# Block 0's logits in a four-layer transformer kernel: half of the shifts on TensorE, half on VectorE

## The chip, the cores and the metric

The kernel runs on one core of a Trainium2 chip. The metric is the device time of one execution in microseconds, the median of the runs. The result is a bfloat16 tensor of 2048 rows by 1024 columns.

## The reference

Four layers work on x (2048 x 1024): attention, gated MLP, attention, gated MLP, each on a layernorm of x and added back to x. Both attention layers use the same weights, and so do both MLP layers.

```python
qkv = layernorm(x) @ wqkv            # 32 heads of 32
idx = pos[:, None] - 2 * arange(8)   # each row sees 8 rows: itself, 2, 4 .. 14 back
logits = einsum("bhsd,bhswd->bhsw", q, k[idx]) * scale   # -1e9 where idx < 0
x = x + einsum("bhsw,bhswd->bhsd", softmax(logits), v[idx]) @ wo
x = x + ((gate * (gate > 0)) * up) @ W_down   # gate, up = layernorm(x) @ W_gate, W_up
```

## The kernel before

The rows are cut into four blocks of 512 (four tiles of 128 rows each). Per layer and block there is a list of stages: layernorm; projections q, k, v; the attention proper; the output projection (wo) with its add to x; for the MLP the gate and up projections and the down projection. Layer indices in the code are 0 to 3, so `proj(0, b)` is the first attention.

**Who does what.** TensorE does all projections, as groups of eight matmuls of 128x512 into one PSUM bank (the pool has eight). ScalarE evicts the projections, takes the sums for the layernorm and normalises. VectorE does the attention, the adds to x and the product of the gated MLP. SP issues nearly all loads. ScalarE issues the writes of q, k and v to DRAM, and GpSimd those of the attention's output and of the 14 halo rows that the next block needs.

**Two layouts.** Projections come out feature-major: partitions are features, columns are rows of x. Attention on VectorE is head-major: partition 32*tq + h holds head h of row tile tq, the free dimension holds 32 features by 128 rows. The change of layout goes through DRAM (`q_d`, `k_d`, `v_d`, written by `evict`, read back in four pieces each as `qhm`, `khm`, `vhm` by `load`). Then `plan_attn` takes, for each of the eight shifts w, one product over 32 features (`mul`, L512) and its sum (`add3`, L522, and `fold`, L529 and L530); then softmax (`soft_a`, `expo`, `soft_b`); then eight steps over features with v (`pv_mul` L563, `pv_add` L571 to L574, which writes `o_d`); then `load_o` (L582) reads the result back, feature-major, as `oT` for the output projection (`plan_wo`, L642, adds at L649).

**Block 0 of layer 0 is special.** Its logits don't go through DRAM. `first_logits` keeps q and k feature-major in SBUF (`q_fm`, `k_fm`); VectorE multiplies each of the eight 128-feature chunks with all eight shifts of k in one instruction (`mul` in `first_logits`, L451), and TensorE sums the 32 features of each head by a matmul with a matrix of ones (`red`, L464; `wide` puts the sums in the right partitions). That is 32 matmuls for chunks 0 to 3 (placed after the first group of q1 by `step(0, 4)`) and 32 for chunks 4 to 7 (placed in block 1's projections by `step(4, 4)`). For this, block 0's projections run in the order q0 v0 k0 v1 q1 k1 (0 and 1 are the halves of 512 features); all others run q0 k0 q1 k1 v0 v1.

**What sets the order.** Instructions of each engine run in the order in which the program emits them. A planner (`Plan`) makes that order: every step gets a due time in us from fixed costs per kind, and steps are emitted by due time. TensorE's steps follow one another (`on_pe`, 0.216 us a matmul). VectorE's attention is one serial list over all blocks (`plan.chain`, each with a time from which it is ready and a cost), and adds and layernorm smalls are put between its entries (`on_dve`). Weight slabs of 512 columns go through a ring of five buffers on SP (`slab`). The due times only set the order; the waits are by semaphores. The six weight slabs of layer 0's projections are held through all four blocks.

In layer 0 the stages on TensorE are: projections of blocks 0, 1 and 2, wo of block 0, projections of block 3, then gate and up of block 0, wo of block 1, and so on.

Of the kernel before, what the change touches and what calls it, by code (L numbers as in the profile page):

```python
# [9 lines left out]
BF16 = mybir.dt.bfloat16  # L10
# [4 lines left out]
P = 128  # L15
# [3 lines left out]
W = 8  # L19
# [6 lines left out]
NEG = -1.0e9  # L26
SLAB = 512
ROW = HALO + BLK
DG = 4
RING = 5  # L30
NG = DH // DG


MM = 0.216
# [85 lines left out]
def kernel(  # L120
# [233 lines left out]
    def plan_proj(L, b, hooks={}):  # L354
# [33 lines left out]
        if L == 0 and b == 0:  # L388
# [4 lines left out]
            for t in range(TPB - 1):  # L393
                for h, (nm, g, j) in ((h, x) for h in range(2) for x in tiles):
                    plan.on_pe(1, mms(nm, g, j, w0[(nm, g)], t, t + 1, KC // 2 * h, KC // 2 * (h + 1)), [w0[(nm, g)]])
                    if h == 1 and j == 2:
                        e = plan.on_pe(2, lambda t=t: first.turn(t + 1))
                        plan.at(e, lambda t=t: first.copies(t + 1))
        order = "q0 k0 q1 k1 v0 v1" if "evict" not in hooks else "q0 v0 k0 v1 q1 k1"
        for nm, g in ((o[0], int(o[1])) for o in order.split()):  # L400
# [20 lines left out]
    def first_logits(st, tm):  # L421
        hold = {}
        Ls = []

        def begin():
            hold["q"] = hm_pool.tile([P, KC, BLK], BF16, tag="q", name="q_fm")
            hold["k"] = hm_pool.tile([P, KC, HALO + BLK], BF16, tag="k", name="k_fm")
            nc.gpsimd.memset(hold["k"][:, :, 0:HALO], 0.0)

        def evict(nm, c, acc, t):  # L430
            def f():
                if nm == "q":
                    nc.scalar.copy(hold["q"][:, c, :], acc()[:])
                    return
                kt = hold["k"]
                nc.scalar.copy(kt[:, c, HALO:HALO + BLK], acc()[:])
                nc.gpsimd.dma_start(_dram(k_d[1], c * P * ROW, [[ROW, P], [1, HALO]]), kt[:, c, BLK:BLK + HALO])
            if nm == "q" and c == 0:
                plan.at(t - 1.0, begin)
            plan.at(t, f)  # L440
            if nm == "k":
                plan.chain.append((lambda: max(t + 0.7, reds.get(c - 4, 0.0) + 0.1), 2.25, mul(c),
                                   (lambda n: tm.__setitem__("logits", n)) if c == KC - 1 else None))

        def mul(c):
            def f():
                if c % 4 < 2:
                    pr = at_pool.tile([P, W, BLK], BF16, tag="pr", name=f"prod_{c}", bufs=2)
                else:
                    pr = tpose.tile([P, W, BLK], BF16, tag="T", name=f"prod_{c}")  # L450
                nc.vector.tensor_tensor(pr[:], _ap(hold["q"], c * BLK, [[0, W], [1, BLK]]),  # L451
                                        _ap(hold["k"], c * ROW + HALO, [[-DIL, W], [1, BLK]]), op=ALU.mult)
                hold[("pr", c)] = pr
            return f

        def red(c0, n):
            def f():
                if c0 == 0:
                    Ls.extend(psum.tile([P, 4, P], F32, tag="acc", name=f"L{wh}") for wh in range(2))
                for c in range(c0, c0 + n):  # L460
                    pr = hold.pop(("pr", c))
                    for wh in range(2):
                        for tq in range(TPB):
                            nc.tensor.matmul(Ls[wh][32 * tq:32 * tq + 32, :, :], lhsT=wide[:, 28 - 4 * c:60 - 4 * c],  # L464
                                             rhs=pr[:, 4 * wh:4 * wh + 4, tq * P:(tq + 1) * P],
                                             start=(c == 0), stop=(c == KC - 1),
                                             skip_group_check=True, tile_position=(0, 32 * tq))
            return f

        def out():  # L470
            st["L"] = at_pool.tile([P, W, P], F32, tag="L", name="L_0_0")
            for wh in range(2):
                nc.scalar.copy(st["L"][:, 4 * wh:4 * wh + 4, :], Ls[wh][:])

        reds = {}

        def step(c0, n):
            def f():
                e = plan.on_pe(1.0 + 2.25 * n, red(c0, n))
                for c in range(c0, c0 + n):  # L480
                    reds[c] = e
                if c0 + n == KC:
                    plan.at(e + T_EV, out)
                    tm["logits_in"] = e + T_EV + 1.5
            return f

        return {"evict": evict, ("q", 1, 0): step(0, 4)}, {("q", 0, 2): step(4, 4)}


    def plan_attn(L, b, ends, st, tm):  # L490

        def load(t, parts):

            def piece(nm, src, row, n, tq):
                def f():
                    if tq == 0:
                        st[nm] = hm_pool.tile([P, DH, n], BF16, tag=nm, name=f"{nm}hm_{L}_{b}")
                    nc.sync.dma_start(st[nm][32 * tq:32 * tq + 32, :, :],
                                      _dram(src[b], tq * P, [[DH * row, H], [row, DH], [1, n]]))
                return f  # L500
            for p in parts:
                for tq in range(TPB):
                    plan.at(t, piece(*p, tq))
                    t += PIECE
            return t - PIECE + T_LAND

        def mul(w):
            def f():
# [79 lines left out]
        chain_tm.append(tm)  # L588

        def qk_ready():  # L590
            t = ends["k"] + 6.0
            if prev:
                t = max(t, prev[-1]["logits"] + 0.5)
            tm["qk_in"] = load(t, (("q", q_d, BLK, P), ("k", k_d, ROW, HALO + P)))
            return tm["qk_in"]

        def v_ready():
            t = ends["v"] + 6.0
            if prev:
                t = max(t, prev[-1]["pv"] + 0.5, tm["qk_in"] + 10.0)  # L600
            return load(t, (("v", v_d, ROW, HALO + P),))

        now = lambda: 0.0
        first = L == 0 and b == 0
        for w in range(0, 0 if first else W):
            plan.chain.append((qk_ready if w == 0 else now, 2.25, mul(w), None))
# [5 lines left out]
            plan.at(t + 0.2, expo)  # L612
            tm["exp"] = t + 2.2

        plan.chain.append(((lambda: tm["logits_in"]) if first else now, 3.0, soft_a, after_a))
# [85 lines left out]
    def plan_down(L, b, st, last):  # L701
# [21 lines left out]
        def add(half, t, c0, n):  # L723
            def f():
                xt = x_tiles[b * TPB + t]
                nc.vector.tensor_tensor(xt[:, c0:c0 + n], accs.pop((t, c0))[:], xt[:, c0:c0 + n], op=ALU.add)  # L726
                r0 = (b * TPB + t) * P
                if end:
                    eng = nc.scalar if t == 1 or (t == TPB - 1 and c0 == SLAB) else nc.sync
                    eng.dma_start(out_dram[r0:r0 + P, c0:c0 + n], xt[:, c0:c0 + n])  # L730
                elif last and half == 1:
                    nc.sync.dma_start(out_dram[r0:r0 + P, :], xt[:])
            return f

        for half in range(2):
# [13 lines left out]
    wo_start = []  # L749
    attn = {}  # L750
    glu = {}
    later_hooks = []

    def proj(L, b):
        st, tm = {}, {}
        if L == 0 and b == 0:
            hooks, later_hooks[:] = (lambda h: (h[0], [h[1]]))(first_logits(st, tm))
# [20 lines left out]
    for i, (nm, g) in enumerate((("q", 0), ("v", 0), ("k", 0), ("v", 1), ("q", 1), ("k", 1))):  # L778
# [77 lines left out]
```

## Time and profile before

| what | value |
|---|---|
| runs | 1623.18, 1622.75, 1622.86 us; median 1622.86 |
| profiled execution | 1622.84 us, its span 1621.1 us |
| TensorE busy, granted clock | 1611.6 us, 1.000 |
| VectorE busy | 1014.6 us |
| ScalarE busy | 458.1 us |
| DMA | 314.83 MB, mean 194 GB/s |

The span runs from the first to the last instruction that the profiler saw, and the execution's time is 1.7 us longer. All times of the trace count from the span's start. A row gives a line of the kernel, the engine, the operation, what is written and read (out<-in), how often, and in the groups the busy time and the mean duration in ns. Busy time of TensorE is pipelined (a matmul is shown as 379 ns and a new one starts every 216 ns), so its duration is read from the chain, where each piece ends where the next begins.

### The profile page before, as it was taken

How to read it: one execution, taken by the hardware profiler on the slowest of the kernel's cores; microseconds unless marked ns; L12 is line 12 of the kernel's file. 1: busy time of each engine (PE TensorE's matmuls, PEld its weight loads, DVE VectorE, ACT ScalarE, POOL GpSimd, SP SyncE). 2: the span in 40 equal slices, each digit the busy share in tenths (PEclk: the TensorE clock that was granted, in tenths of full speed). 3: DMA queues.
4: the chain of work that ended last, by engine and by line, in shares of the span. 5: the costliest groups of instructions: out<-in, count | busy, mean ns of one | idle time of the engine just before them, and what ended most of it. 6: DMA issues, size and time to landing. Idle time of an engine off the chain costs nothing.

```text
span 1621.1 us, 19223 instructions
## 1 busy us (share of the span) xinstructions
PE 1611.6 (99%) x7641; PEld 740.6 (46%) x7690; DVE 1014.6 (63%) x1256; ACT 458.1 (28%) x735; POOL 109.3 (7%) x174
## 2 busy tenths in 40 slices
PE   9999999999999999999999999999999999999999
PEld 5444444444444444444444444444444444444444
DVE  4576999989989069960699616986989212211211
ACT  6564421304131241312413251133011311221110
POOL 3221000001001100011000110000000000000000
PEclk9999999999999999999999999999999999999999
DMA  8799798597866988669876699599846655565452
GB/s 240 163 199 192 191 218 210 167 217 193 219 173 211 223 206 208 188 200 234 202 198 196 213 223 226 158 279 240 216 154 194 172 182 162 176 173 165 156 167 67
DMA packets 444203, 314.83 MB, mean 194 GB/s; under 512 B 195504, under 2 KB 438608, under 8 KB 444112
## 3 DMA queue, kind: packets, MB, share of 16 engines
q1 hardware_dynamic: 414944, 281.39, 66.7%
q10 hardware_dynamic: 24368, 23.40, 4.7%
q0 software_dynamic: 4800, 8.80, 1.8%
q8 instruction: 60, 0.98, 0.3%
q14 instruction: 31, 0.25, 0.1%
HBM read 261.77 MB, written 36.05 MB: 184 GB/s over the span
## 4 chain that ended last, share of the span: by engine, by line
PE 99%; DMA 0%; DVE 0%; issue 0%; SPq 0%; POOL 0%; DVEq 0%; POOLq 0%
PE acc_g L672 24%; PE acc_u L672 24%; PE dacc L718 24%; PE acc_v L364 7%; PE acc_k L364 7%; PE acc_wo L642 7%; PE acc_q L364 7%; DMA x<-in_A_x_dram 0%; PE L L464 0%; DVE bst L294 0%; POOL rstd L318 0%; DVE xn_all L323 0%; DVE x L726 0%; SPq L785 0%; DVE xnT L331 0%
## 5 line engine op out<-in xcount | busy, mean ns | idle before, releaser
L672 PE MATMUL acc_u<-xnT,wu 128*128 128x512 bf16 x1792 | 423.3, 379 | 0.0
L672 PE MATMUL acc_g<-xnT,wg 128*128 128x512 bf16 x1792 | 423.3, 379 | 0.0
L718 PE MATMUL dacc<-wd,hT 128*128 128x512 bf16 (+1 forms) x1787 | 386.4, 376 | 1.7
L687 DVE TENSOR_TENSOR hT<-acc_u,r 128x512 bf16<-128x512 f32 x224 | 154.1, 688 | 323.9 <-PE acc_u L672 318.3
L679 ACT ACTIVATE r<-acc_g 128x512 bf16<-128x512 f32 x224 | 133.3, 596 | 711.9 <-PE acc_g L672 700.3
L718 PEld LDWEIGHTS <-hT 128*128 128x128 bf16 x1820 | 178.1, 98 | 209.0
L672 PEld LDWEIGHTS <-wu 128*128 128x128 bf16 x1792 | 175.3, 98 | 211.4
L672 PEld LDWEIGHTS <-wg 128*128 128x128 bf16 x1792 | 175.3, 98 | 211.5
L512 DVE TENSOR_TENSOR pr<-qhm,khm 128x4096 bf16<-128x4096 bf16 x56 | 127.9, 2284 | 30.7 <-DMA khm<-k_d 30.6
L563 DVE TENSOR_TENSOR pvt<-a,vhm 128x4096 bf16<-128x4096 bf16 x64 | 146.2, 2285 | 0.2
L522 DVE TENSOR_TENSOR l<-l,pr 128x1024 f32<-128x1024 f32 x112 | 136.8, 1221 | 2.2
L726 DVE TENSOR_TENSOR x<-dacc,x 128x512 bf16<-128x512 f32 (+1 forms) x65 | 43.2, 681 | 126.1 <-PE dacc L718 125.9
L364 PE MATMUL acc_v<-xnT,wv 128*128 128x512 bf16 x512 | 112.0, 379 | 0.0
L642 PE MATMUL acc_wo<-wo,oT 128*128 128x512 bf16 x496 | 111.0, 379 | 0.8
L364 PE MATMUL acc_k<-xnT,wk 128*128 128x512 bf16 x384 | 84.8, 379 | 0.0
L219 ACT ACTIVATE xn_all<-x 128x1024 bf16<-128x1024 bf16 x60 | 63.3, 1055 | 73.8 <-DVE x L649 71.0
L571 DVE TENSOR_TENSOR pvt<-pvt 128x2048 bf16<-128x2048 bf16 x64 | 78.1, 1221 | 1.3
L373 ACT CAST stage_q<-acc_q 128x512 bf16<-128x512 f32 x56 | 32.0, 582 | 162.1 <-PE acc_q L364 153.3
L642 PEld LDWEIGHTS <-oT 128*128 128x128 bf16 x512 | 50.1, 98 | 60.4
L364 PEld LDWEIGHTS <-wv 128*128 128x128 bf16 x512 | 50.1, 98 | 60.2
L244 ACT ACTIVATE xn_all<-x,nb,rstd 128x1024 bf16<-128x1024 bf16 x60 | 71.9, 1233 | 14.2 <-DVE nb L238 11.2
L574 POOL DMA_DIRECT2D o_d<-ohm x64 | 35.2, 550 | 599.7 <-DVE ohm L573 581.7
(76 smaller groups left out, 883.1 us busy)
## 6 DMA issues: line engine op xcount, KB each, us to landing
wg<-in_B_W_gate_dram SPq DMA_DIRECT2D x56, 1024.0 KB, 7.2
wu<-in_B_W_up_dram SPq DMA_DIRECT2D x56, 1024.0 KB, 5.4
wd<-in_B_W_down_dram SPq DMA_DIRECT2D x48, 1024.0 KB, 6.4
wo<-in_A_wo_dram SPq DMA_DIRECT2D x16, 1024.0 KB, 6.9
wv<-in_A_wqkv_dram SPq DMA_DIRECT2D x10, 1024.0 KB, 5.7
wk<-in_A_wqkv_dram SPq DMA_DIRECT2D x9, 1024.0 KB, 5.0
vhm<-v_d SPq DMA_DIRECT2D x32, 284.0 KB, 7.0
v_d<-stage_v ACTq DMA_DIRECT2D x32, 256.0 KB, 6.8
```

What stands on the lines that cost most here:

```text
L219: nc.scalar.activation(junk, xt[:], ACT.Identity, accum_out=st[:, 0, t % 2:t % 2 + 1])
L244: nc.scalar.activation(hold["xn"][:, t, :], x_tiles[b * TPB + t][:], ACT.Identity, scale=rstd[:, i:i + 1], bias=nb[:, i:i + 1])
L364: nc.tensor.matmul(acc[:, t0 * P:t1 * P], lhsT=w["t"][:, kc, j * P:(j + 1) * P], rhs=xnT[(L, b)][:, t0:t1, kc, :], start=(kc == 0), stop=( ...
L512: nc.vector.tensor_tensor(pr[:], st["q"][:], _ap(st["k"], HALO - DIL * w, [[HALO + P, DH], [1, P]]), op=ALU.mult)
L522: nc.vector.tensor_tensor(l[:], pr[:, 0:8] if i == 0 else l[:], pr[:, 8 * i + 8:8 * i + 16], op=ALU.add)
L563: nc.vector.tensor_tensor(tt[:], a_bc, v_sh, op=ALU.mult)
L571: nc.vector.tensor_tensor(tt[:, 0:4], tt[:, 0:4], tt[:, 4:8], op=ALU.add)
L642: nc.tensor.matmul(acc[:], lhsT=st["oT"][:, c, t, :], rhs=ws[half]["t"][:, c, :], start=(c == 0), stop=(c == KC - 1))
L672: nc.tensor.matmul(acc[:], lhsT=w["t"][:, kc, (j % 4) * P:(j % 4 + 1) * P], rhs=xnT[(L, b)][:, :, kc, :], start=(kc == 0), stop=(kc == KC ...
L679: nc.scalar.activation(r[:], hold.pop(("g", j))[:], ACT.Relu)
L687: nc.vector.tensor_tensor(st["hT"][:, j, :], hold.pop(("u", j))[:], hold.pop(("r", j))[:], op=ALU.mult)
L718: nc.tensor.matmul(accs[(t, c0)][:], lhsT=st["hT"][:, j, t * P:(t + 1) * P], rhs=w["t"][:, jl, c0 - half * SLAB:c0 - half * SLAB + n], sta ...
```

## The change

TensorE sums only the shifts 0 to 3 of block 0's logits (`NPE = 4`): products of half the size, and 16 matmuls in place of 32 in each of the two `red` steps, into one PSUM bank in place of two. The shifts 4 to 7 of block 0 go the head-major way on VectorE: q and k of block 0 are also written to DRAM, and loaded as `qhm` and `khm` with due times 2 us apart. Block 0's projections run in the common order q0 k0 q1 k1 v0 v1; `step(0, 4)` stands after the first group of k1, `step(4, 4)` after v0. `q_fm` and `k_fm` now lie in buffers of the transposed layernorm's pool, without a halo per chunk (the columns in front of a chunk are the chunk before; the rows that this touches are masked). The wo of block 0 moves from before the projections of block 3 to behind q0 and k0 of block 3. The due times of its `oT` loads, its slabs' first load time (30 to 60) and those of v's load change with it. In the last layer, rows of x are stored by halves of 512 columns in all blocks, where before only the last block did that.

```diff
-        order = "q0 k0 q1 k1 v0 v1" if "evict" not in hooks else "q0 v0 k0 v1 q1 k1"
+        for nm, g in (("q", 0), ("k", 0), ("q", 1), ("k", 1), ("v", 0), ("v", 1)):
...
         def evict(nm, c, acc, t):
             def f():
+                f0 = FRONT if nm == "k" else 0
+                fm = hold[nm]
+                nc.scalar.copy(fm[:, f0 + c * BLK:f0 + (c + 1) * BLK], acc()[:])
+                if c % 2 == 0:
+                    return
...
+                    nc.scalar.dma_start(_dram(q_d[0], r0 * BLK, [[BLK, P], [P * BLK, 2], [1, BLK]]), src)
...
+                nc.scalar.dma_start(_dram(k_d[0], r0 * ROW + HALO, [[ROW, P], [P * ROW, 2], [1, BLK]]), src)
+                nc.gpsimd.dma_start(_dram(k_d[1], r0 * ROW, [[ROW, P], [P * ROW, 2], [1, HALO]]), src[:, :, BLK - HALO:BLK])
...
-                nc.vector.tensor_tensor(pr[:], _ap(hold["q"], c * BLK, [[0, W], [1, BLK]]),
-                                        _ap(hold["k"], c * ROW + HALO, [[-DIL, W], [1, BLK]]), op=ALU.mult)
+                nc.vector.tensor_tensor(pr, _ap(hold["q"], c * BLK, [[0, NPE], [1, BLK]]),
+                                        _ap(hold["k"], FRONT + c * BLK, [[-DIL, NPE], [1, BLK]]), op=ALU.mult)
...
-                    for wh in range(2):
-                        for tq in range(TPB):
+                    for tq in range(TPB):
...
-        return {"evict": evict, ("q", 1, 0): step(0, 4)}, {("q", 0, 2): step(4, 4)}
+        return {"evict": evict, ("k", 1, 0): step(0, 4), ("v", 0, 3): step(4, 4)}
...
         def qk_ready():
+            if first:
+                load(ends["q"] + 6.0, (("q", q_d, BLK, P),), 2.0)
+                tm["qk_in"] = load(ends["k"] + 6.0, (("k", k_d, ROW, HALO + P),), 2.0)
+                return tm["qk_in"]
...
-        for w in range(0, 0 if first else W):
+        for w in range(NPE if first else 0, W):
...
-            step = 3.0 if first else PIECE
+            step = min(PIECE, max(2.0, (st["wo_at"] - 9.5 - T_LAND - t) / 3))
...
-        ws = [slab(wo_v[:, :, h * SLAB:(h + 1) * SLAB], f"wo_{L}_{b}_{h}", 30.0) for h in range(2)]
+        ws = [slab(wo_v[:, :, h * SLAB:(h + 1) * SLAB], f"wo_{L}_{b}_{h}", 60.0) for h in range(2)]
...
-                if end:
-                    eng = nc.scalar if t == 1 or (t == TPB - 1 and c0 == SLAB) else nc.sync
+                if last:
+                    eng = nc.scalar if end and (t == 1 or (t == TPB - 1 and c0 == SLAB)) else nc.sync
...
-            hooks = later_hooks.pop() if later_hooks else {}
+            hooks = {("k", 0, 3): lambda: wo(0, 0)} if L == 0 and b == NB - 1 else {}
...
-        if b == NB - 1:
-            wo(0, 0)
         proj(0, b)
```

More of the change, by code (lines that the diff above doesn't have):

```diff
@@ L28 @@
 ROW = HALO + BLK
+FRONT = 16
 DG = 4
@@ L31 @@
 NG = DH // DG
+NPE = 4
 MM = 0.216
@@ L398, in plan_proj @@
                         plan.at(e, lambda t=t: first.copies(t + 1))
-        order = "q0 k0 q1 k1 v0 v1" if "evict" not in hooks else "q0 v0 k0 v1 q1 k1"
-        for nm, g in ((o[0], int(o[1])) for o in order.split()):
+        for nm, g in (("q", 0), ("k", 0), ("q", 1), ("k", 1), ("v", 0), ("v", 1)):
             if L == 0:
@@ L425, in begin @@
         def begin():
-            hold["q"] = hm_pool.tile([P, KC, BLK], BF16, tag="q", name="q_fm")
-            hold["k"] = hm_pool.tile([P, KC, HALO + BLK], BF16, tag="k", name="k_fm")
-            nc.gpsimd.memset(hold["k"][:, :, 0:HALO], 0.0)
+            hold["q"] = tpose.tile([P, KC * BLK], BF16, tag="T", name="q_fm")
+            hold["k"] = tpose.tile([P, FRONT + KC * BLK], BF16, tag="T", name="k_fm")
+            nc.gpsimd.memset(hold["k"][:, 0:FRONT], 0.0)
         def evict(nm, c, acc, t):
             def f():
+                f0 = FRONT if nm == "k" else 0
[3 more added lines that the diff above has]
+                    return
+                src = fm[:, f0 + (c - 1) * BLK:f0 + (c + 1) * BLK].rearrange("p (c n) -> p c n", c=2)
+                r0 = (c - 1) * P
                 if nm == "q":
-                    nc.scalar.copy(hold["q"][:, c, :], acc()[:])
+                    nc.scalar.dma_start(_dram(q_d[0], r0 * BLK, [[BLK, P], [P * BLK, 2], [1, BLK]]), src)
                     return
-                kt = hold["k"]
-                nc.scalar.copy(kt[:, c, HALO:HALO + BLK], acc()[:])
-                nc.gpsimd.dma_start(_dram(k_d[1], c * P * ROW, [[ROW, P], [1, HALO]]), kt[:, c, BLK:BLK + HALO])
+                nc.scalar.dma_start(_dram(k_d[0], r0 * ROW + HALO, [[ROW, P], [P * ROW, 2], [1, BLK]]), src)
+                nc.gpsimd.dma_start(_dram(k_d[1], r0 * ROW, [[ROW, P], [P * ROW, 2], [1, HALO]]), src[:, :, BLK - HALO:BLK])
             if nm == "q" and c == 0:
@@ L441, in evict @@
             if nm == "k":
-                plan.chain.append((lambda: max(t + 0.7, reds.get(c - 4, 0.0) + 0.1), 2.25, mul(c),
-                                   (lambda n: tm.__setitem__("logits", n)) if c == KC - 1 else None))
+                plan.chain.append((lambda: max(t + 0.7, reds.get(c - 4, 0.0) + 0.1), 1.2, mul(c), None))
         def mul(c):
             def f():
[L447 to L450, printed above, removed]
-                nc.vector.tensor_tensor(pr[:], _ap(hold["q"], c * BLK, [[0, W], [1, BLK]]),
-                                        _ap(hold["k"], c * ROW + HALO, [[-DIL, W], [1, BLK]]), op=ALU.mult)
+                if c % 2 == 0:
+                    hold["pr"] = at_pool.tile([P, 2, NPE, BLK], BF16, tag="pr", name=f"prod_{c}", bufs=2)
+                pr = hold["pr"][:, c % 2]
+                nc.vector.tensor_tensor(pr, _ap(hold["q"], c * BLK, [[0, NPE], [1, BLK]]),
+                                        _ap(hold["k"], FRONT + c * BLK, [[-DIL, NPE], [1, BLK]]), op=ALU.mult)
                 hold[("pr", c)] = pr
@@ L458, in f @@
                 if c0 == 0:
-                    Ls.extend(psum.tile([P, 4, P], F32, tag="acc", name=f"L{wh}") for wh in range(2))
+                    Ls.append(psum.tile([P, NPE, P], F32, tag="acc", name="Lps"))
                 for c in range(c0, c0 + n):
                     pr = hold.pop(("pr", c))
-                    for wh in range(2):
-                        for tq in range(TPB):
[L464 to L467, printed above, removed]
+                    for tq in range(TPB):
+                        nc.tensor.matmul(Ls[0][32 * tq:32 * tq + 32, :, :], lhsT=wide[:, 28 - 4 * c:60 - 4 * c],
+                                         rhs=pr[:, :, tq * P:(tq + 1) * P],
+                                         start=(c == 0), stop=(c == KC - 1),
+                                         skip_group_check=True, tile_position=(0, 32 * tq))
             return f
@@ L471, in out @@
             st["L"] = at_pool.tile([P, W, P], F32, tag="L", name="L_0_0")
-            for wh in range(2):
-                nc.scalar.copy(st["L"][:, 4 * wh:4 * wh + 4, :], Ls[wh][:])
+            nc.scalar.copy(st["L"][:, 0:NPE, :], Ls[0][:])
         reds = {}
@@ L478, in f @@
             def f():
-                e = plan.on_pe(1.0 + 2.25 * n, red(c0, n))
+                e = plan.on_pe(1.0 + 1.13 * n, red(c0, n))
                 for c in range(c0, c0 + n):
@@ L483, in f, with load @@
                     plan.at(e + T_EV, out)
-                    tm["logits_in"] = e + T_EV + 1.5
             return f
-        return {"evict": evict, ("q", 1, 0): step(0, 4)}, {("q", 0, 2): step(4, 4)}
+        return {"evict": evict, ("k", 1, 0): step(0, 4), ("v", 0, 3): step(4, 4)}
     def plan_attn(L, b, ends, st, tm):
-        def load(t, parts):
+        def load(t, parts, gap=PIECE):
             def piece(nm, src, row, n, tq):
@@ L503, in load @@
                     plan.at(t, piece(*p, tq))
-                    t += PIECE
-            return t - PIECE + T_LAND
+                    t += gap
+            return t - gap + T_LAND
         def mul(w):
@@ L590, in qk_ready @@
         def qk_ready():
-            t = ends["k"] + 6.0
-            if prev:
-                t = max(t, prev[-1]["logits"] + 0.5)
+            if first:
+                load(ends["q"] + 6.0, (("q", q_d, BLK, P),), 2.0)
+                tm["qk_in"] = load(ends["k"] + 6.0, (("k", k_d, ROW, HALO + P),), 2.0)
+                return tm["qk_in"]
+            t = max(ends["k"] + 6.0, prev[-1]["logits"] + 0.5)
             tm["qk_in"] = load(t, (("q", q_d, BLK, P), ("k", k_d, ROW, HALO + P)))
@@ L597, in v_ready @@
         def v_ready():
-            t = ends["v"] + 6.0
+            t = max(ends["v"] + 6.0, tm["qk_in"] + 10.0)
             if prev:
-                t = max(t, prev[-1]["pv"] + 0.5, tm["qk_in"] + 10.0)
+                t = max(t, prev[-1]["pv"] + 0.5)
             return load(t, (("v", v_d, ROW, HALO + P),))
@@ L604, in plan_attn @@
         first = L == 0 and b == 0
-        for w in range(0, 0 if first else W):
-            plan.chain.append((qk_ready if w == 0 else now, 2.25, mul(w), None))
+        for w in range(NPE if first else 0, W):
+            plan.chain.append((qk_ready if w in (0, NPE) and (w == 0) != first else now, 2.25, mul(w), None))
             for i in range(3):
@@ L613, in after_a @@
             tm["exp"] = t + 2.2
-        plan.chain.append(((lambda: tm["logits_in"]) if first else now, 3.0, soft_a, after_a))
+        plan.chain.append((now, 3.0, soft_a, after_a))
         plan.chain.append((lambda: tm["exp"], 4.0, soft_b, None))
@@ L727, in f @@
                 r0 = (b * TPB + t) * P
-                if end:
-                    eng = nc.scalar if t == 1 or (t == TPB - 1 and c0 == SLAB) else nc.sync
+                if last:
+                    eng = nc.scalar if end and (t == 1 or (t == TPB - 1 and c0 == SLAB)) else nc.sync
                     eng.dma_start(out_dram[r0:r0 + P, c0:c0 + n], xt[:, c0:c0 + n])
-                elif last and half == 1:
-                    nc.sync.dma_start(out_dram[r0:r0 + P, :], xt[:])
             return f
@@ L751 @@
     glu = {}
-    later_hooks = []
     def proj(L, b):
@@ L756, in proj @@
         if L == 0 and b == 0:
-            hooks, later_hooks[:] = (lambda h: (h[0], [h[1]]))(first_logits(st, tm))
+            hooks = first_logits(st, tm)
         else:
-            hooks = later_hooks.pop() if later_hooks else {}
+            hooks = {("k", 0, 3): lambda: wo(0, 0)} if L == 0 and b == NB - 1 else {}
         attn[(L, b)] = plan_attn(L, b, plan_proj(L, b, hooks), st, tm)
@@ L777 @@
     held = hT_pool.tile([P, FC, BLK], BF16, tag="hT", name="wqk_0")
-    for i, (nm, g) in enumerate((("q", 0), ("v", 0), ("k", 0), ("v", 1), ("q", 1), ("k", 1))):
+    for i, (nm, g) in enumerate((("q", 0), ("k", 0), ("q", 1), ("k", 1), ("v", 0), ("v", 1))):
         col0 = "qkv".index(nm) * D + g * SLAB
```

## The prediction

> **What bounds the kernel now.** I read the page first, then TensorE's waits, then the chain of waits around the changed stage.
>
> ```profile
> PE 1611.6 (99%) x7641; PEld 740.6 (46%) x7690; DVE 1014.6 (63%) x1256; ACT 458.1 (28%) x735; POOL 109.3 (7%) x174
> ...
> PE 99%; DMA 0%; DVE 0%; issue 0%; SPq 0%; POOL 0%; DVEq 0%; POOLq 0%
> ```
>
> TensorE is the whole chain that ended last. Busy time alone would prove little, so the list of what it waited for is next; it is complete:
>
> ```profile
> PE warm L289 <- POOL neg_half L177: 1.4, 1, 1.4
> PE acc_q L364 <- DMA wqk<-in_A_wqkv_dram: 0.7, 1, 0.7
> PE tp L328 <- DVE xn_all L323: 0.7, 1, 0.7
> PE acc_q L364 <- ACT xnT L331: 0.5, 2, 0.2
> ```
>
> All four lie in the first 16 us. After that TensorE never waits, so the time is the sum of its instructions. An edit that takes TensorE work away gains it in full, and any new wait of TensorE is lost in full. The chain, stretch 35 to 65 us (start, duration, what):
>
> ```profile
> 39.13 1.73 PE acc_q L364 x8
> 40.86 1.84 PE L L464 x32
> 42.70 5.29 PE acc_q L364 x24
> 47.98 6.91 PE acc_k L364 x32
> 54.89 5.18 PE acc_q L364 x24
> 60.07 1.84 PE L L464 x32
> 61.91 1.83 PE acc_q L364 x8
> ```
>
> A projection group of 8 matmuls takes 1.73 us, so 0.216 each. Thirty-two logit matmuls take 1.84: four run side by side, 8 x 0.216 = 1.73, and 0.11 is left over. The 24 matmuls behind take 5.29 instead of 5.18, another 0.11. So a block costs 0.22 for entering and leaving, and 0.054 per matmul.
>
> **TensorE's work.** Each of the two L464 blocks falls from 32 to 16 matmuls: 4 x 0.216 = 0.86 off each, 1.73 in all. The 0.22 stays, as there are still two blocks. If the leftover shrank too it would be 1.84. I take 1.73. The moved output projection and the new order q, k, v are the same matmuls.
>
> **Weights of block 0.** The six loads are issued in the same order and kind; only their names change. The trace's landings by place are about 13.2, 16.4, 23.8, 28.1 and 31.7 for places two to six; their first uses are 18.4, 25.3, 32.2, 40.2 and 48.2. Margin 5 us or more: nothing. The wo slabs are loaded from about 70 us on instead of 41 and needed past 150: nothing. Twelve more output DMAs on SP, at half 0 of the last layer, wait for VectorE's add; L732's waits were 3.4 us at most, and a weight slab behind them is issued some 20 us before use: nothing. The zero halo DMAs on POOL go from 8 of 0.556 to 4 of 0.72: nothing.
>
> **First products.** They now need a k chunk, evicted by ScalarE between the layernorm passes of block 1. ScalarE is full from 19 to 39 us. Of its work there, the passes take 2.27 each (x4), the norms 1.15 (x4), a cast 0.5, a DMA issue 0.45. New in it are four more issues before chunk 4 of k, for q and k go to DRAM (1.8 us). In its new order it comes to the passes at 20.1 (19.0 and two issues), then three passes, four casts and one issue bring chunk 3 of k out at 20.1 + 6.8 + 2.0 + 0.5 = 29.4, and the half product (the row below, half of L451's 2286) ends by 31.0. TensorE asks at 33.95. Behind that come the fourth pass, four norms, eight casts and four issues, 2.3 + 4.6 + 4.0 + 1.8, so chunk 7 is out near 42.1 and its product ends at 45.3; TensorE asks for chunks 4 to 7 from 47.1 on. Margins 2.9 and 1.8 us. Nothing, with at most 2 us if ScalarE falls that much further behind. While ScalarE is late, PSUM's eight banks cover it: the worst lag that I get is 6.7 us, four groups.
>
> ```profile
> L571 DVE TENSOR_TENSOR pvt<-pvt 128x2048 bf16<-128x2048 bf16 x64 | 78.1, 1221 | 1.3
> ```
>
> **The other four shifts, on VectorE.** These go in the hole of VectorE's timeline:
>
> ```profile
> 113.31 0.43 DVE L573 TENSOR_TENSOR ohm<-pvt 128x512 bf16<-128x512 bf16 x1
> ...
> 136.30 2.29 DVE L512 TENSOR_TENSOR pr<-qhm,khm 128x4096 bf16<-128x4096 bf16 x1 [14.78 <-DMA khm<-k_d]
> ...
> 143.79 2.28 DVE L512 TENSOR_TENSOR pr<-qhm,khm 128x4096 bf16<-128x4096 bf16 x1
> ```
>
> Block 0's attention ended at 113.74 and block 1's logits began at 136.30. One head-major shift takes 143.79 - 136.30 = 7.49.
>
> Start: the last k write is issued near 42.6. Such writes landed in 3.9 to 7.0 (v_d at that time), so by about 48. Then SP issues four khm pieces (one x tile between), 2.5 us; khm landings are 4.6 to 11.8, median 8.8. Last landing 53.6 to 63.9; I take the median, 59.3. Behind the waiting L512 stand the layernorm smalls of block 2 on VectorE, and behind those, on ScalarE, norms and evictions of block 1. PSUM's eight banks give TensorE some 12 us (seven groups of 1.73) before that reaches it.
>
> Length: 4 x 7.49 = 30.0; two rounds of layernorm smalls in between, 1.9; softmax as it ran, 62.85 to 73.56, 10.7; the eight pv steps as they ran, 74.24 to 113.74, 39.5, and another 0.9 of smalls. Sum 83.0, so block 0's attention ends at 142.3 instead of 113.7. Block 1's logits, which began at 136.3, begin then: 6 us later. Block 1's pv ended at 255.7 and its wo begins at 291.5, so 36 us of slack cover that.
>
> **The output projection of block 0.** This is where the cover is thin. It moves behind q0 and k0 of block 3, 64 matmuls or 13.81 us, and takes its eight adds, four oT loads and the layernorm of block 0 along. In before it began at 139.72; now at 139.72 - 1.73 + 13.81 = 151.8. It needs the first oT piece then, and the other three 3.45 us apart. The o_d write landed 4.1 us after the last pv step (113.74 to 117.8), so 146.4. SP's oT rows:
>
> ```profile
> 122.82 1.01 SPq L582 DMA_DIRECT2D oT<-o_d  x2
> 130.91 0.56 SPq L498 DMA_DIRECT2D khm<-k_d  x1
> 133.63 2.60 SPq L582 DMA_DIRECT2D oT<-o_d  x2
> ```
>
> These four landed 3.1 to 4.7 after their issue: 149.5 to 151.1, so 0.7 to 2.3 us to spare. The lower bound of the cost is zero; a gain is excluded since TensorE waited for nothing here. The upper: khm at 63.9 makes the piece land at 154.1 to 155.7, a stall of up to 3.9; and SP issued the first oT only 5 us after o_d was in, a hold that would add 5 if it came again. I take zero, as the medians give. Queued behind the wait are, on TensorE, everything; on SP, v pieces of block 1 and the first gate slab, used after 190.
>
> [...]
>
> **The layernorm behind it.** In before the last transpose landed at 179.9, 26.4 us after wo's end (153.53). Now 165.6 + 26.4 = 192.0, and the gate matmuls begin at 194.97 - 1.73 = 193.2. That is an upper bound, as VectorE's adds then sat up to 7.7 us behind logits that had started late. Cost zero; 2 us if it were slower by three.
>
> **Sum.** Profiled execution 1622.84 (span 1621.1 and 1.7 around it); the median of runs is 1622.86. 1622.84 - 1.73 = 1621.1.
>
> **Rivals.** (1) The forecast, no new wait: 60%, 1621.1. (2) oT is late by 0.5 to 4 us, as the far ends of the khm and landing rows allow: 22%, 1621.6 to 1625.1. It turns into a loss past a stall of 1.73. (3) Slower: the last khm piece of block 0 is held on SP, as block 1's was (three pieces by 110.2, the fourth at 130.91, TensorE unhurt then, since wo's data was ahead). VectorE's chain is serial, so each us goes through to wo. From a landing at 63 the kernel is slower than before, from 66 by over 0.2%; held by 12 us, the stall is about 10 and the time 1631. For it: such a hold is in the trace. Against: no oT stands before khm now. 10%. (4) TensorE waits for a product in one of the two blocks, up to 2 us: 6%, 1621.1 to 1623.1. (5) The saving isn't made, as the block's cost doesn't go with its matmuls: 2%, 1622.8; the 0.216 steps speak against it.
>
> About 0.2%, 3.2 us, is what a measurement of this kernel can tell from no change. Faster than that (below 1619.6) needs more than the change takes from TensorE: 1%. Slower (above 1626.1) is rival 3 and a tail of 2: 12%. The rest, 87%, is within. The range 1620.7 (a saving of 1.84 and the 0.3 us by which the runs scatter) to 1624.3 leaves out rival 3 and the upper part of 2, about 15%, and 2% below.
>
> **What would show it.** In the chain, two rows L464 x16 of about 0.97; TensorE's list of waits unchanged; wo's first matmul at 151.8 with no wait on DMA oT; VectorE's hole before 136 gone and its first L512 near 59; block 1's first L512 near 142. Wrong, if the list of waits gains a row on oT, prod or xnT; its length is then the error.

## The result, and the profile after

The changed kernel takes 1630.47 us (median of 6 runs, 1627.28 to 1634.61) against 1622.76 for the kernel before: a ratio of 1.0049, 95% interval 1.0035 to 1.0063. It is slower, by 7.7 us; 1621.1 was forecast. The profiled execution took 1631.80 us, its span 1630.1. The six executions spread over 7.3 us, those of the kernel before over 0.7; every wait below is read from one profiled execution of its kernel and need not be the same in the others.

On the page of the changed kernel, the busy times and the chain that ended last:

```profile
PE 1613.5 (99%) x7609; PEld 740.4 (45%) x7658; DVE 1036.2 (64%) x1284; ACT 459.2 (28%) x734; POOL 108.9 (7%) x170
...
PE 95%; DMA 2%; DVE 1%; issue 0%; POOL 0%; SPq 0%; ACT 0%; DVEq 0%; POOLq 0%
```

TensorE still shows 99% busy, yet it is 95% of the chain and no longer 99%. What it waited for (total, times, longest, in us):

```profile
PE acc_q L366 <- DMA xnT<-xn_all: 6.9, 2, 4.0
PE warm L291 <- POOL neg_half L179: 1.4, 1, 1.4
PE tp L330 <- DVE xn_all L325: 0.8, 1, 0.8
PE acc_q L366 <- DVE xnT L333: 0.6, 1, 0.6
PE acc_q L366 <- ACT xnT L333: 0.5, 2, 0.2
```

Behind the first 16 us one row is new: twice TensorE stood before the first q group of a block and waited for its transposed layernorm. No row names oT or prod. Where this lies, in the chain (start, duration, what), first from 16 to 70 us:

```profile
33.95 0.98 PE Lps L468 x16
34.92 5.29 PE acc_k L366 x24
...
47.11 0.98 PE Lps L468 x16
```

and from 90 to 200 us:

```profile
89.15 10.14 DMA xnT<-xn_all
...
99.43 8.75 PE acc_q L366 x32
...
137.29 9.28 DMA xnT<-xn_all
...
146.71 8.75 PE acc_q L366 x32
155.47 6.91 PE acc_k L366 x32
162.37 0.22 PE acc_wo L646
```

The saving on the logits is made: two blocks of 0.98 where there were two of 1.84. But q0 of block 2 starts at 99.43, when its transposes land at 99.3, and q0 of block 3 at 146.71, when its transposes land at 146.6. And both q0 slabs take 8.75 us instead of 6.91. The table by stretches says why (columns: us; busy and count of PE, PEld, DVE, ACT, POOL; granted clock; DMA share; GB/s):

```profile
101.00:103.00 2.00, 2.00 (x6) 0.76 (x5) 0.88 (x2) 1.57 (x3) 0.00 (x0) 0.50 0.86 213
```

Behind each wait the clock granted is one half for a while, and a matmul starts every 0.427 us instead of 0.216. The account of the profiled execution: 1622.84 - 1.73 + 6.9 of waits + 2 x 1.84 at half clock = 1631.7, against 1631.80.

### The profile page after: what moved, and what is told of

Same layout as the page of the kernel before. It is cut to its first block, busy times and chain, and to the rows that moved or that the text cites. A ratio compares the mean times of both kernels' runs of the same rounds, so it can differ in the third digit from the quotient of the medians.

```text
span 1630.1 us, 19236 instructions
## 1 busy us (share of the span) xinstructions
PE 1613.5 (99%) x7609; PEld 740.4 (45%) x7658; DVE 1036.2 (64%) x1284; ACT 459.2 (28%) x734; POOL 108.9 (7%) x170
## 4 chain that ended last, share of the span: by engine, by line
PE 95%; DMA 2%; DVE 1%; issue 0%; POOL 0%; SPq 0%; ACT 0%; DVEq 0%; POOLq 0%
PE acc_u L676 24%; PE acc_g L676 24%; PE dacc L722 24%; PE acc_wo L646 7%; PE acc_k L366 6%; PE acc_q L366 6%; PE acc_v L366 6%; DMA xnT<-xn_all 1%; DVE l L524 0%; DMA khm<-k_d 0%; DMA v_d<-stage_v 0%; DVE pr L514 0%; DMA x<-in_A_x_dram 0%; POOL rstd L235 0%; DVE bst L296 0%
## 5 line engine op out<-in xcount | busy, mean ns | idle before, releaser
L514 DVE TENSOR_TENSOR pr<-qhm,khm 128x4096 bf16<-128x4096 bf16 x60 | 137.0, 2284 | 35.7 <-DMA x<-in_A_x_dram 21.5
L524 DVE TENSOR_TENSOR l<-l,pr 128x1024 f32<-128x1024 f32 x120 | 146.6, 1222 | 2.6
L366 PE MATMUL acc_k<-xnT,wk 128*128 128x512 bf16 x512 | 113.3, 379 | 0.0
L366 PE MATMUL acc_v<-xnT,wv 128*128 128x512 bf16 x384 | 84.2, 379 | 0.0
L366 PEld LDWEIGHTS <-wk 128*128 128x128 bf16 x512 | 50.0, 98 | 60.4 <-issue 0.4
```

Source lines behind the costliest of these rows:

```text
L366: nc.tensor.matmul(acc[:, t0 * P:t1 * P], lhsT=w["t"][:, kc, j * P:(j + 1) * P], rhs=xnT[(L, b)][:, t0:t1, kc, :], start=(kc == 0), stop=( ...
L514: nc.vector.tensor_tensor(pr[:], st["q"][:], _ap(st["k"], HALO - DIL * w, [[HALO + P, DH], [1, P]]), op=ALU.mult)
L524: nc.vector.tensor_tensor(l[:], pr[:, 0:8] if i == 0 else l[:], pr[:, 8 * i + 8:8 * i + 16], op=ALU.add)
```

## The experiments

There are three theories. **A**: there are two causes, VectorE's late start makes the norms of block 2 late, and moving wo makes block 3's projections start before their transposes. **B**: both waits come from VectorE's late chain. **C**: it is the traffic of the trip through DRAM, and SyncE (SP) held in front of the transposes. In what follows, "waits" are TensorE's after the first 16 us, from the profile of the run.

### Four parts, each by itself

The move of wo alone, put into the kernel before:

```diff
+            if L == 0 and b == NB - 1:
+                hooks = {("k", 0, 3): lambda: wo(0, 0)}
...
-        if b == NB - 1:
-            wo(0, 0)
         proj(0, b)
```

> The kernel before, with one edit: wo of block 0 stands behind q0 and k0 of block 3. TensorE sums all eight shifts as before. Theory A: the transposes of block 3, which landed at 148.1, are now needed at 139.7, so TensorE waits there by up to 8 us and half clock follows: 1626 to 1633 us. Theory B: no effect, 1622.8 us.

Measured: 1631.44, ratio 1.0054 (1.0042 to 1.0066). This one edit costs as much as the whole change. TensorE's list of waits for it begins:

```profile
PE acc_q L364 <- DMA xnT<-xn_all: 6.3, 1, 6.3
```

and its chain has

```profile
140.56 5.69 DMA xnT<-xn_all
...
146.39 9.73 PE acc_q L364 x32
```

In the chain of the kernel before, q0 of block 3 had the whole of wo ahead of it:

```profile
139.99 10.74 PE acc_wo L642 x49
...
153.53 6.91 PE acc_q L364 x32
```

Its transposes landed at 148.1, 5.4 us ahead of 153.53. With wo moved behind q0 and k0, q0 is due at 140, and the transposes land at 146.25.

Next, the changed kernel without the four head-major shifts (the shifts 4 to 7 of block 0 count as logits of zero) and without their trip through DRAM, and the same with the trip made but not used (the last line below, with its like for k, is left out in the first of the two only):

```diff
-        for w in range(NPE if first else 0, W):
+        for w in range(W if first else 0, W):
...
-                    nc.scalar.dma_start(_dram(q_d[0], r0 * BLK, [[BLK, P], [P * BLK, 2], [1, BLK]]), src)
```

> The changed kernel, with block 0's shifts 4 to 7 left out: their logits are set to zero, and q and k of block 0 are neither written to DRAM nor loaded. Everything else of the change stays, the move of wo too. Theory A: TensorE's two waits have two causes. Block 2's (3 us) comes from VectorE's late start: the layernorm smalls of block 2 stand in its queue behind the first head-major product, which waits for khm. Block 3's (4 us) comes from the move of wo: block 3's projections begin 13.8 us earlier, and its transposes landed at 148.1 in the kernel before, 10 us later than they are now needed. A expects no wait at block 2 and still a wait at block 3: 1622 to 1629 us. Theory B: both come from VectorE's late chain. It expects no wait and 1621.1 us.

> As e2_tensor_cut_alone, but q and k of block 0 make their trip through DRAM (written and loaded, and not used). Theory A: as e2, 1622 to 1629 us, with no wait at block 2. Theory C: the traffic of the trip and SP's held queue make the transposes of block 2 late, not VectorE. C expects a wait of 2 to 4 us at block 2 and 4 us or more above e2.

Measured: without both, 1627.9, ratio 1.003 (1.0019 to 1.0041); with the trip, 1633.78, ratio 1.0055 (1.0036 to 1.0074). The eight executions with the trip spread from 1624.2 to 1637.67, and the profiled one is the slowest of them. The waits of the first:

```profile
PE acc_q L366 <- DMA xnT<-xn_all: 3.2, 1, 3.2
```

and of the second:

```profile
PE acc_q L366 <- DMA xnT<-xn_all: 11.8, 2, 6.2
```

Without the trip block 2 isn't waited for; block 3 still is. With the trip, and with no work of VectorE added, block 2 is waited for by 6.2 us, more than in the changed kernel and more than C had expected (2 to 4). Its norms ended at 83.7, before those of the changed kernel (89.1), yet SP issued the first transpose only at 88.85, when a k write of ScalarE had landed (88.77):

```profile
88.85 6.91 SPq L252 DMA_TRANSPOSE xnT<-xn_all  x2
```

So B falls, and the trip's transfers alone are enough to make block 2 late, as C has it. In the changed kernel itself VectorE's lateness is there too: its second transpose waited for its norm, which ended at 89.13 (84.86 in the kernel before), was issued at 89.15 and took 10.1 us to land, against 6.4 in the kernel before.

Last, the transposes of blocks 2 and 3 due 0.5 us behind the norms instead of 8:

```diff
-            late_ln(0, b + 1, plan.pe + 9.0, 0.5 if b == 0 else 8.0)
+            late_ln(0, b + 1, plan.pe + 9.0, 0.5)
```

> The changed kernel, with the transposes of blocks 2 and 3 due 0.5 us after their norms in place of 8, which moves them ahead of later loads in SP's queue. Theory A: block 3's wait gets shorter or goes, since two held khm pieces then stand behind its transposes; block 2's changes by under 1 us, since there the norms themselves are late: 1624 to 1628 us. Theory B: no change, 1630 us.

Measured: 1632.61, ratio 1.0062 (1.005 to 1.0074).

```profile
PE acc_q L366 <- DMA xnT<-xn_all: 9.0, 1, 9.0
```

A had expected the opposite, a shorter wait at block 3 and the same one at block 2. Block 2's wait is gone, though its norms ended at 88.7, nearly as late as in the changed kernel: the first transpose was issued at 83.57 instead of 86.81, and the second landed 6.7 us after its issue, at 95.4. So late norms alone don't make block 2 late. What each of the two gives in the changed kernel these runs don't divide. And nothing is gained: block 3's wait has become 9.0, since its transposes land at 146.9, much as in the changed kernel (146.6). The two waits are not a sum. Each transpose is a deadline; what TensorE loses at the first it needn't lose at the second.

### Is the deadline all? Layernorm earlier

The layernorm of blocks 2 and 3 begun 8 us earlier, transposes at once, their rows loaded 12 us earlier. Of the four runs, the first is the kernel before with wo moved, and the earlier layernorm for block 3 alone; the second is the kernel before, with nothing else; the third is the changed kernel; the fourth is the changed kernel, for block 3 alone. The line as it stands in the second and third:

```diff
+            late_ln(0, b + 1, plan.pe + (9.0 if b == 0 else 1.0), 0.5)
```

> The kernel before with two edits: the output projection of block 0 behind the q and k slabs of block 3, and block 3's layernorm, rows and transposes earlier. Deadline theory: moving the output projection costs 8.6 us only through the transposes of block 3, so the time is that of the kernel before, 1622.8 (1622.4 to 1623.3). Rival (the move costs by itself): 1626 or more.

> The kernel before with the layernorm, rows and transposes of blocks 2 and 3 earlier, nothing else. There TensorE waits on no transpose, so every theory expects 1622.8 (within 0.4); if it is faster, the earlier layernorm is worth something by itself and the reading of the first of these runs has to be reduced by it.

> The changed kernel, with the layernorm of blocks 2 and 3 begun 8 us earlier in the plan, its transposes issued at once (lag 0.5 in place of 8) and the input rows of these blocks loaded 12 us earlier. Deadline theory (the lost time is wholly the late landing of the transposes of blocks 2 and 3 against projections that start earlier): no row of TensorE waiting on xnT, the saving of 1.73 stands, 1622.8 - 1.7 = 1621.1 (1620.8 to 1621.5). Rival (moving the output projection or loading through the trip costs TensorE something else): the waits on xnT go and the time stays above 1623. Second rival (the earlier layernorm collides with the loads of the head-major copies, and the transposes land as late as before): a wait of 3 us or more is left, over 1625.

> The changed kernel, with the earlier layernorm, rows and transposes for block 3 alone. Deadline theory: the wait at block 2 stays at 3 us and is no longer taken back at block 3, since no deadline stands there any more: 1621.1 + 3.05 + 1.7 for the half clock behind it = 1625.9. Rival (the wait at block 2 costs nothing, being VectorE's lateness only): 1621.1.

Measured: 1622.80 (ratio 1.0, 0.9991 to 1.0009) with wo moved; 1622.70 (0.9999, 0.999 to 1.0007) without. In the chain of the first, wo stands behind q0 and k0 and TensorE waits nowhere:

```profile
125.59 13.81 PE acc_v L364 x64
139.40 6.91 PE acc_q L364 x32
146.31 6.91 PE acc_k L364 x32
153.21 13.81 PE acc_wo L642 x64
```

So moving wo costs nothing by itself: all of its 8.6 us go through block 3's transposes, and the earlier layernorm is worth nothing where nobody waits. In the changed kernel the same edit misses its forecasts of 1621.1 and 1625.9: 1633.25 for both blocks (1.0064, 1.0051 to 1.0077), waits 6.2 at block 3 and 2.4 for evictions; 1635.8 for block 3 alone (1.0074, 1.006 to 1.0088), 13.8 at block 2, whose transposes SP reached only at 100.45, behind x loads of block 3 that were being held.

Why SP is held, in its timeline in the changed kernel (start, duration, what):

```profile
110.55 21.98 SPq L500 DMA_DIRECT2D khm<-k_d  x4
132.63 8.79 SPq L252 DMA_TRANSPOSE xnT<-xn_all  x2
```

Four khm loads of block 1 take 22 us to issue. The first pair of norms of block 3 was done at 127.3, but the last khm piece was issued at 131.99, released by the landing (131.97) of a k write that ScalarE had issued for block 2. The load doesn't read that data. In the trace's records all transfers of SP and ScalarE tell of their landing on the same eight semaphores (100 to 102 and 104 to 108): the k write used 106, and the khm piece waits on 106 and uses it next. The first transpose, issued at 132.63 and no longer waiting for its norms, takes 4.5 us to issue and 9.5 to land; the second follows at 137.29.

### Taking loads from in front of the transposes

Loads of qhm and khm of blocks 0 and 1 issued by GpSimd; the same with early layernorm; early layernorm with khm of block 1 behind block 3's transposes on SP; that with block 0's loads on GpSimd:

```diff
-                    nc.sync.dma_start(st[nm][32 * tq:32 * tq + 32, :, :],
+                    (nc.gpsimd if L == 0 and b < 2 and nm != "v" else nc.sync).dma_start(st[nm][32 * tq:32 * tq + 32, :, :],
...
+            if L == 0 and b == 1:
+                t = 108.0 - TPB * PIECE
```

> The changed kernel, with one edit: the loads of qhm and khm of blocks 0 and 1 are issued by GpSimd instead of SyncE; layernorm and lag as in the changed kernel. Queue theory (the transposes are late because SyncE, in order, is held in front of them by head-major loads that wait on ScalarE's stores): khm of block 0 lands before 62 instead of 66.1, no wait at block 2; block 3's transposes are issued when the norms are done, at about 127 and 131 instead of 132.6 and 137.3, and land at 137 to 141, so that the wait at block 3 is 0 to 3 us: 1621.1 to 1626. Rival (VectorE and ScalarE make the norms late, SyncE only follows): block 2's norms still end at 89 and the wait at block 3 stays at 4 us or more: 1630. Second rival (GpSimd takes so long over these loads that khm is later still): over 1631.

> The earlier layernorm of blocks 2 and 3 as in g1, the rows of these blocks loaded earlier still (20 and 55 in the plan), and the loads of qhm and khm of blocks 0 and 1 on GpSimd. Queue theory: SyncE reaches the transposes as soon as the norms are done, no row of TensorE waiting on xnT, 1621.1 (1620.8 to 1621.6). Rival (norms late behind products that wait on khm, or evictions behind norms on ScalarE): 2 us or more of waits stay, over 1623.

> The earlier layernorm of blocks 2 and 3 as in g1, their rows loaded earlier still, and the four khm loads of block 1 put behind the transposes of block 3 on SyncE's queue; no load on GpSimd. Queue theory: the transposes of block 3 no longer stand behind a load that waits (12 us of it in g1, 137.4 against 124.5), so they land before 137 and the wait at block 3 is gone; block 2 keeps what g1 had there (1.3 us): 1621.1 to 1623. Rival (the norms are what is late): block 3's wait stays over 3 us, 1626 or more.

> As h4, and the loads of qhm and khm of block 0 alone on GpSimd, so that neither khm stands in front of a transpose on SyncE. Queue theory: 1621.1 (1620.8 to 1621.6), no wait on xnT at either block. Rival (GpSimd's loads of block 0 land later than SyncE's, VectorE begins its head-major products later, and the norms of block 2 behind them are later): a wait at block 2 of 1 us or more, over 1623.

Measured: 1635.51, 1641.49, 1633.31, 1635.19 (ratios 1.0078, 1.0121, 1.0062, 1.0077, each within 0.0017). All four forecasts of the queue theory missed. GpSimd is no way out: in the first, khm landed at 65.8 instead of 66.1, 8 us and more after issue; and ScalarE's evictions stood 19 us in four waits for their own writes to land, so that block 2's norms ended at 95.8 instead of 89.1. Besides xnT (5.8 and 7.2), TensorE waited 4.4 us for evictions in the first and 4.8 in the second, 2.4 us for products in the second and third and 2.8 in the fourth, where evictions took another 3.9 and oT 3.0. The third is the telling one: its transposes land at 99.0 and 139.7, no row of xnT from DMA is left, and the time is no better. Its longest wait is

```profile
PE acc_wo L649 <- DMA oT<-o_d: 4.6, 1, 4.6
```

The forecast's second rival has appeared, behind the deadline that hid it. Part of this wait is of the run's own making: khm of block 0 landed at 71.5, 5.4 us later than in the changed kernel, and VectorE's serial part behind it wrote its last result at 156.7 instead of 149.0.

### Three deadlines, one behind the other

To see whether oT is a deadline of its own: wo one slab later with the rest as changed (j2); layernorms of blocks 2 and 3 earlier by 3 and 8 us, transposes at once, rows of block 3 at 55, the wo slabs at 98, khm of block 1 and vhm of block 1 moved back (j3); both (j1).

```diff
-            hooks = {("k", 0, 3): lambda: wo(0, 0)} if L == 0 and b == NB - 1 else {}
+            hooks = {("q", 1, 3): lambda: wo(0, 0)} if L == 0 and b == NB - 1 else {}
...
+            late_ln(0, b + 1, plan.pe + (9.0, 6.0, 1.0)[b], 0.5)
```

> The changed kernel, with the output projection of block 0 one slab further back (behind q0, k0 and q1 of block 3 instead of q0 and k0). Two-deadline theory: the first deadline, the transposes of block 3 landing at about 146.6, is untouched, and oT (first piece 152.3 in the changed kernel) was in time before; so the same waits at blocks 2 and 3 and the same time, 1630.5 (1628 to 1634). Rival (the place of the output projection is itself what costs): several us of difference.

> The changed kernel with layernorm of blocks 2 and 3 begun 3 and 8 us earlier, transposes at once, block 3's rows loaded at 55 in the plan, the wo slabs at 98, khm of block 1 behind block 3's transposes and vhm of block 1 behind oT; the output projection stays behind q0 and k0 of block 3. Two-deadline theory: the waits on xnT go, the output projection would begin at 151.8 and oT's first piece lands at 152 to 156: TensorE waits 0.5 to 5 us on oT, and with 1.7 for a half clock where the wait is over 3 us the time is 1621.6 to 1627.8. Rival (the early edits alone make oT late; without x at 20 in the plan there is no wait): 1621.1.

> As j3, with the output projection one slab further back, so that it would begin at 158.7. Two-deadline theory: no wait on xnT and none on oT; the saving of 1.73 stands: 1621.1 (1620.8 to 1622). Rival (a further wait follows, for instance the gate of the next layer on xnT of layer 1, whose transposes landed 20.2 us after the output projection's end and would land at about 193 against a gate at 195): 1622 to 1626.

Measured: j2 1629.66 (1.004, 1.0026 to 1.0053), like the changed kernel; j3 1624.19 (1.0013, 1.0004 to 1.0022); j1 1628.76 (1.0037, 1.0024 to 1.0049). In j3 2.1 us of waits for xnT are left, in two of 1.4 and 0.7 with no half clock behind them (the granted clock of the profiled execution is 1.000), and oT's first piece lands at 153.91, just as wo begins at 153.96. So j3's time lies in its forecast for another reason than the one forecast, a wait on oT. j1 missed its forecast of 1621.1; in it a third deadline shows, the one that its expectation named as rival:

```profile
PE acc_g L681 <- DMA xnT<-xn_all: 4.3, 1, 4.3
```

```profile
193.20 7.29 DMA xnT<-xn_all
200.62 3.54 PE acc_g L681 x8
```

(the list of waits, and the chain). With wo one slab later the next layer's transposes land at 200.5, after the gate is due at 196.3.

Then the loads of vhm and of the wo slabs behind block 2's transposes (k1; k2 with block 3's layernorm 2 us later), and vhm two before and two behind (l1, the last line of the diff, with `jump` 69.5 for vhm of block 0):

```diff
-            t = max(ends["v"] + 6.0, tm["qk_in"] + 10.0)
+            t = max(ends["v"] + 6.0, tm["qk_in"] + 10.0, 70.0 if first else 0.0)
...
-                    t += gap
+                    t = max(t + gap, jump) if tq == 1 else t + gap
```

> As j3, with the vhm loads of block 0 (70 in the plan) and the wo slabs (76) put behind the transposes of block 2, so that no load stands between two transposes. Queue theory: the second transposes of block 2 land before 96 (97.8 in j3) and those of block 3 before 137.5 (140.0): no wait on xnT. Then oT decides: its first piece landed at 153.9 in j3 against an output projection that can begin at 151.8, a wait of 0 to 2.1 us: 1621.1 to 1623.2. Rival (the transposes are slow for the traffic itself): the waits of 2.1 us stay, 1623.5 to 1624.2.

> As k1, with block 3's layernorm begun 2 us later in the plan. If the 2.7 us by which VectorE's chain of block 0 ended later in j3 (147.6 against 144.9 in the changed kernel) came from its waits for GpSimd's rstd (3.1 us, up to 2.5 at a time), the chain ends earlier here and oT is in time: 1621.1 to 1622. Otherwise as k1.

> As j3, with the wo slabs at 60 again, and of the vhm loads of block 0 two before and two behind block 2's transposes. Two-deadline theory: transposes as in k1 (before 96 and before 138), no wait on xnT; vhm lands before 104, VectorE begins its products with v at 103.5 to 105.7, its part of block 0 ends at 145 to 147.6, and oT's first piece lands at 151.5 to 153.9 against an output projection that can begin at 151.8: 1621.1 to 1623.2, below or at the kernel before. Rival (something is late again, the norms or vhm, whatever the order of the loads, since the loads of 40 to 110 fill the DMA engines): 1624 or more.

Measured: k1 1631.94 (1.0059, 1.0042 to 1.0076), k2 1633.08 (1.0061, 1.0043 to 1.0079), l1 1625.04 (1.0013, 1.0003 to 1.0022). In k1 and k2 the transposes landed early enough (92.5 and 137.0 in k1, no wait on them), but vhm came at 112.2 and 114.7, VectorE's products with v began at 112.45 and 114.90 instead of 105.65 in j3, and wo waited (in k1):

```profile
PE acc_wo L651 <- DMA oT<-o_d: 5.3, 1, 5.3
```

In l1 both transposes are in time (95.1, 135.7) and vhm too. One wait remains:

```profile
PE acc_wo L651 <- DMA oT<-o_d: 2.1, 1, 2.1
```

```profile
145.52 3.77 DMA o_d<-ohm
...
149.35 4.35 DMA oT<-o_d
...
153.75 15.67 PE acc_wo L651 x64
```

(the list of waits, and the chain of l1). wo could have begun at 151.63, where k0 ended; the forecast had 151.8. VectorE's last write lands at 149.29, the first oT piece at 153.70. The 64 matmuls take 15.67 instead of 13.81, as the clock is halved behind this wait (0.50 granted from 154 to 156 us); l1's forecast, up to 1623.2, had the wait but not the half clock.

All of it adds up, from the forecast of 1621.1:

| kernel | waits, us | half clock, us | sum | profiled |
|---|---|---|---|---|
| changed | xnT 6.9 | 3.7 | 1631.7 | 1631.80 |
| transposes at once | xnT 9.0 | 1.6 | 1631.7 | 1631.88 |
| j2 | xnT 6.8 | 3.6 | 1631.5 | 1631.53 |
| j3 | xnT 2.1 | none | 1623.2 | 1623.55 |
| j1 | xnT 3.0, gate 4.3 | 1.8 | 1630.2 | 1630.43 |
| k1 | oT 5.3, eviction 2.2 | 2.1 | 1630.7 | 1630.96 |
| l1 | oT 2.1 | 1.9 | 1625.1 | 1625.04 |

The forecast's sum of work is right to 0.4 us in every row; what it lacked is the waits. j3 and l1 win back most of what the change lost, but neither beats the kernel before. By this sum a kernel breaks even at 1.7 us of waits with no half clock, and reaches the forecast if oT lands 2.1 us earlier with l1's transposes; neither was tried.

## Why the prediction was wrong

The result lies above its range and past its bound for slower, to which it gave 12%.

**What held.** The saving: 0.98 and 0.98, 24 matmuls at 5.29 behind the first, as worked out. The products: the half product ended at 30.65 (by 31.0), the last at 44.8 (45.3). The place of wo, 151.8, is met in l1 (151.63) where nothing else stalls. The rest of oT's way: 4.1 from the last pv step to the landed write (4.0), 3.1 to 4.7 from issue to landing (3.2 in the changed kernel, 4.35 in l1).

**The step that failed first: "It moves behind q0 and k0 of block 3 ... and takes its eight adds, four oT loads and the layernorm of block 0 along."** It followed what moves back and not what moves forward. Taking 13.8 us of wo from in front of q0 of block 3 makes q0 due at 138 instead of 153.5, and the trace of before had its transposes landing at 148.1. That was up to 10 us of stall to be read from rows at hand; the wo move alone measured 6.3 of wait and 8.6 of time. Margins were worked out for the moved step and for its followers, but none for the work that took its place.

**The second: "PSUM's eight banks give TensorE some 12 us ... before that reaches it", as the cover of a late khm.** It named the layernorm smalls behind the waiting VectorE and the evictions behind those, but not what the smalls lead to: block 2's transposes, which had 7.0 us to spare in before (landed 91.3, asked for at 98.3) and landed at 99.3 after (asked for at 96.5). The norms ended 4.3 us later and the last transpose took 3.8 longer to land. The run with the trip and no shifts shows that VectorE's lateness isn't even needed for it, SP's hold does it; how much each gave in the changed kernel stays open. And the landing taken, 59.3 with 63.9 as the far end, was 66.1: the pieces were issued at 52.67, 53.25, 56.66 and 60.90, the last two held for v writes to land. The mis-sized term is the issue of the four, forecast for 48 to 50.5 and measured to 61.4; the landing took 5.0 to 5.9, less than the 8.8 taken. The trace of before had 21 us of such a hold (rival 3 quotes it), and "no oT stands before khm now" was no reason against it.

**Rivals 2 and 3.** The condition of 3 came true, a landing from 66 on, yet its price, wo's wait for oT, was not paid: xnT's waits had pushed wo to 162.4, past oT's first landing at 152.3. Rival 2 is real behind them, 2.1 us in l1. VectorE's part was over-estimated in length (83.0; 66.29 to 144.93 is 78.6) and began 7.0 late, so its end, 144.9 for a forecast 142.3, is near by luck. None of the rivals names xnT; only the last sentence does, and it has the length of the row as the error: the row is 6.9, the error of the profiled execution 10.7, and the half clock makes up 3.7.

**The clock.** The sum has no term for a lower clock; the one granted to the kernel before was 1.000. Behind each of the two new waits one half was granted for a while, which cost 1.84 a time. The 1.7 that two expectations take for it (the earlier layernorm for block 3 alone, and j3), and j3's condition of a wait over 3 us, are shown by no run: the chains have 1.6 to 3.0 behind such waits, and 2.9 was enough here, 2.1 in l1.

**The layernorm behind wo.** 26.4 us were taken as a bound; 20.2 measured. There were 7.4 to spare in the changed kernel. In j1 the same distance was 25.0, near the bound, and there it is what binds.

## What to carry to other kernels

When a stage is moved back on the engine that sets the time, list what moves forward into its place and check each input's landing in the trace against the new start: the loss is there, not at the moved stage. Where an engine is full, late inputs are deadlines: the time follows the latest and hides the rest, so removing one wait shows the next and a sum of waits overstates what a repair can gain. SP's queue carried a hold from one transfer to all behind it (two transposes stood behind 22 us of khm loads), so a transfer with a deadline wants no load in front of it that can wait.

## What the runs showed of the hardware

**Half clock came behind gaps as short as 2.1 us.** Behind idle times of TensorE (from the modelled end of one matmul to the start of the next) of 2.1 (l1, the wait for oT), 2.4 (j2, block 2) and 2.9 us (changed, block 2) the matmuls took 1.86 (64 in 15.67 instead of 13.81), 1.80 (32 in 8.71 instead of 6.91) and 1.84 us longer (32 in 8.75). In the changed kernel the granted clock was 0.50 from 99.94 to 103.35 us and, behind the wait of 4.0, from 147.73 to 151.14; from 100.20 to 103.19 a matmul started every 0.427 us. In the chains, the matmuls behind waits of 3.2 (without shifts and trip) to 9.0 us (transposes at once) took 1.6 to 3.0 us longer.

After 2.2 us in k1 nothing like it shows: its profiled execution is 0.3 us above the sum, which has only the 2.1 behind oT. Nor after waits of 1.7 or less in j1 and of 1.4 in j3 (0.2 and 0.4 above their sums). So length alone doesn't decide between 2.1 and 2.2 us; what does was not shown.

**A load waited for a store it had nothing to do with.** In the changed kernel the fourth khm piece of block 1 was issued 0.02 us after a k write of block 2 landed (131.97). The third was issued 0.01 us after a q write of block 2 landed (125.08). In this way four khm loads took 22 us of SP's queue, and two transposes behind them could not start.
